# Layer 1's second mixer product as 8 × 7 Strassen products instead of 16 plain ones

## The chip, the cores and the metric

The kernel runs on one core of a Trainium2 chip. The time is the device time of one execution in microseconds (us); the time before is the median of three runs. A profiled execution has a span (first to last instruction), a little shorter than its own time.

Five engines work side by side, each on its own queue in order: PE (TensorE) multiplies, with its weight loads listed as PEld; DVE (VectorE), ACT (ScalarE) and POOL (GpSimd) work element by element; SP issues DMA transfers. SBUF is the memory on the chip and PSUM the one that PE writes its sums to.

## The reference

x has 2048 tokens × 512 channels. Twice over, attention is added to x and then a token mixer, both on a layer norm of x:

```python
x = x + _A_ref(_layernorm(x), wq, wk, wv, wo)
x = x + _B_ref(_layernorm(x), w1, b1, w2, b2)

def _B_ref(x, w1, b1, w2, b2):
    h = _layernorm(x)                                # (B, S, D)
    u = jnp.einsum("bsd,sf->bdf", h, w1) + b1        # (B, D, F)
    u = _gelu(u)
    y = jnp.einsum("bdf,fs->bds", u, w2) + b2        # (B, D, S)
    return y.transpose(0, 2, 1)
```

S is 2048, D 512, F 1792. The second mixer product is out[s,d] = sum over f of w2[f,s]·u[f,d]: 16 token tiles of 128 and 14 inner tiles of 128.

## The kernel before

All is float32. A matmul operand is split into a high part (rounded to PE's fast format, fp32r) and a low part (the rest); of each product three terms are kept: high·high, high·low and low·high. So every split is a cast (high, mostly ACT) and a subtraction (low, DVE or POOL), and every tile pair costs three matmuls.

**First mixer product** (u before the gelu). Its w1 tiles come in 128 KB loads (`load1`, SP, L1160), are cast on ACT (L1168) and get their low part on POOL (L1170). The sums go from PSUM into the tiles `ua0` to `ua13` by DVE adds (L1191). `rest` does what is left of it after the attention: behind each product `following` splits the w1 tile three ahead and loads the one seven ahead. Once an `ua` tile is complete, its gelu follows on ACT (L1389), the cast of the result on ACT (L1390), and the low part on DVE (L1394). These pieces stand between the products, by a count of turns. At its opening `rest` also issues the first two loads of w2 on SP.

**Second mixer product.** For each of the 16 token tiles, `second` does 14 × 3 = 42 matmuls of 128×128 weights against 512 columns (L1423) into one PSUM bank. w2 comes in halves of a token tile, 128×896, 448 KB each (`load2`, L1403), two buffers; `split2` casts (ACT, L1411) and subtracts (DVE, L1412) one half at a time, three buffers. One DVE instruction adds the bank and b2 to x (L1429), and SP writes the tile out.

The order of instructions on each engine is the order in which this code calls them; nothing reorders it later.

Of the kernel before, what the change touches and what calls it, by code (L numbers as in the profile page):

```python
# [8 lines left out]
F32 = mybir.dt.float32  # L9
# [9 lines left out]
P = 128  # L19
# [28 lines left out]
NP = 8  # L48
NMORE = 4
NQ = 2  # L50

VROWS = ((KR, 0, HALF - KR), (HALF + KR, HALF - KR, DH - HALF + KR))
SHIFT = 0.515625
# [13 lines left out]
def kernel(  # L67
# [993 lines left out]
    class Mixer:  # L1061
# [21 lines left out]
        def open(self):  # L1083
            n = self.l
            self.opened = True
            self.ap = pool(f"uacc{n}")
            self.wp = pool(f"w1p{n}")
            self.hp = pool(f"hp{n}")
            self.uacc = [self.ap.tile([P, D], F32, tag=f"ua{f}", name=f"ua{n}_{f}") for f in range(NF)]

        def norm(self, ts_):

# [152 lines left out]
        def rest(self, att):  # L1245
# [83 lines left out]
            att.pp.release()  # L1329
            self.open_u()  # L1330
            warm(AF.Gelu_apprx_tanh)
            self.load2(0)
            self.load2(1)
            for k, pu in enumerate(going):
                self.product(pu, start=False, stop=False)
                self.following()
                if k in (5, 7):
                    self.split2((k - 5) // 2)
            late, begun, turns = [], [], iter(range(2 * NF))

# [32 lines left out]
            for g in late:  # L1373
                self.gelu(g)
                self.gelu_rest(g)
            self.split2(2)
            self.hp.release()
            self.wp.release()
            self.ap.release()

        def open_u(self):
            n = self.l
            self.up = pool(f"up{n}", side="right")
            self.w2p = pool(f"w2p{n}", side="right")
            self.u = [self.up.tile([P, 2, D], F32R, tag=f"u{f}", name=f"u{n}_{f}") for f in range(NF)]

        def gelu(self, f):
            tmp = self.uacc[f]
            nc.scalar.activation(tmp, tmp, AF.Gelu_apprx_tanh, bias=b1c[:, f : f + 1])  # L1389
            nc.scalar.copy(self.u[f][:, 0, :], tmp)  # L1390

        def gelu_rest(self, f):
            tmp = self.uacc[f]
            nc.vector.tensor_tensor(self.u[f][:, 1, :], tmp, f32(self.u[f][:, 0, :]), op=ALU.subtract)  # L1394


# [37 lines left out]
            self.split2(2 * s + 4)  # L1434

        def close(self):
            self.w2p.release()
            self.up.release()

# [110 lines left out]
    for layer in range(2):  # L1550
# [4 lines left out]
        if more:  # L1555
            warm(AF.Exp)
            proj = Proj(layer + 1)
        for s in range(NKT):
            b = s // 4 - 1
            if more and s >= 1:  # L1560
                proj.stat(s - 1)
            if more and s >= 4 and s % 4 == 0:
                proj.spreads(tiles(b))
                proj.scales(tiles(b))
                proj.norm(tiles(b))
            if more and s == NKT - 1:
# [5 lines left out]
            if not more:  # L1572
                nc.sync.dma_start(xout[:, s, :], x[s])
                continue
# [121 lines left out]
```

## Time and profile before

| | |
|---|---|
| Median of 3 runs | 2527.39 us (2527.11 to 2529.62) |
| The profiled execution, its own time | 2527.02 us |
| Its span; outside the span | 2525.3 us; 1.7 us |
| Mean granted TensorE clock | 0.999 |
| Busy: PE / ACT / DVE / POOL | 2503.4 / 2106.1 / 1507.8 / 151.6 us |
| Layer 1's second product: first matmul to the end of the last | 2369.13 to 2521.51 us |

All times below are of this profiled execution, from the start of its span. The shares over the whole span say little here: the attention fills most of it, and the change is in the last 6%. That stretch is to be read by itself: its chain of waits, its groups of instructions, and the busy time of each engine in each part of it.

### The profile page before, as it was taken

What the parts mean: (1) busy time and instruction counts of PE and PEld (TensorE: products, weight loads), DVE (VectorE), ACT (ScalarE), POOL (GpSimd) and SP (SyncE); (2) the same over time, 40 slices, a digit from 0 to 9 for tenths busy, and PEclk for the clock granted to TensorE, in tenths of its full rate; (3) what the DMA queues carried; (4) which work ended last, traced back from release to release, by engine and by line L of the source; (5) the groups of instructions that cost most, each with busy time, mean ns of one, the idle gap of its engine ahead of it and who ended that gap; (6) DMA issues with size and microseconds to landing.
All of it is one profiled execution on the core that took longest, in us unless ns stands there. A gap on an engine that the chain in (4) does not pass through costs nothing. (4 is left out here: it accounts for less than half of the span.)

```text
span 2525.3 us, 41882 instructions
## 1 busy us (share of the span) xinstructions
PE 2503.4 (99%) x16158; PEld 1238.5 (49%) x16158; DVE 1507.8 (60%) x2406; ACT 2106.1 (83%) x2350; POOL 151.6 (6%) x239
## 2 busy tenths in 40 slices
PE   9999999999999999999999999999999999999999
PEld 6444334444444444588864433344444444436887
DVE  6565566667666776464445662666676566755532
ACT  6999999999999999653349999999999999995511
POOL 5000000000000000241000000000000000002300
PEclk9999999999999999999999999999999999999999
DMA  3221201111111110134422210111111111102343
GB/s 116 74 66 41 65 27 41 31 41 31 39 31 39 31 41 28 43 111 115 125 77 83 58 49 29 31 39 30 41 31 39 31 43 33 39 22 66 110 124 95
DMA packets 168275, 139.33 MB, mean 55 GB/s; under 512 B 17506, under 2 KB 132224, under 8 KB 167808
## 3 DMA queue, kind: packets, MB, share of 16 engines
q1 hardware_dynamic: 168064, 136.52, 18.5%
q8 instruction: 131, 2.15, 0.4%
q14 instruction: 80, 0.66, 0.1%
HBM read 95.57 MB, written 24.12 MB: 47 GB/s over the span
## 5 line engine op out<-in xcount | busy, mean ns | idle before, releaser
L906 ACT ACTIVATE p<-sc 128x1024 f32<-128x1024 f32 x1479 | 1434.4, 1048 | 68.1 <-PE sc L896 67.4
L912 PE MATMUL acc<-p,vaug 128*32 128x512 f32 x8192 | 1005.4, 599 | 0.4 <-DVE q L519 0.4
L904 DVE COPY p<-sc 128x1024 f32<-128x1024 f32 x569 | 696.7, 1224 | 475.1 <-PE sc L896 422.7
L896 PE MATMUL sc<-qs,kst 51*128 51x512 f32 x4096 | 690.2, 433 | 10.8 <-SPq L618 5.0
L906 ACT ACTIVATE p<-p 128x1024 f32<-128x1024 f32 x569 | 615.2, 1081 | 12.3 <-DVE p L904 7.3
L896 PEld LDWEIGHTS sc<-qs,kst 51*128 51x128 f32 x4096 | 335.8, 184 | 580.4 <-ACT p L906 395.4
L912 PEld LDWEIGHTS acc<-p,vaug 128*32 128x32 f32 x8192 | 218.6, 109 | 485.5 <-issue 470.0
L1423 PE MATMUL py<-u,w 128*128 128x512 f32 x1344 | 307.6, 390 | 0.0
L1423 PEld LDWEIGHTS py<-u,w 128*128 128x128 f32 x1344 | 251.8, 188 | 52.4
L1411 ACT CAST w<-w2r 128x896 fp32r<-128x896 f32 x64 | 60.3, 945 | 186.3 <-PE py L1423 178.1
L1183 PE MATMUL pu<-hb,w 128*128 128x512 f32 x768 | 204.5, 407 | 0.0
L1170 POOL TENSOR_TENSOR w<-w1r,w 128x256 fp32r<-128x256 f32 x90 | 73.5, 825 | 1648.6 <-ACT w L1168 1648.2
L1183 PEld LDWEIGHTS pu<-hb,w 128*128 128x128 f32 x768 | 136.2, 188 | 58.4 <-issue 31.7
L814 DVE COPY ev<-acc 128x512 f32<-128x512 f32 x64 | 43.9, 686 | 166.5 <-PE acc L912 166.5
L1412 DVE TENSOR_TENSOR w<-w2r,w 128x896 fp32r<-128x896 f32 x64 | 72.3, 1130 | 112.3 <-ACT w L1411 112.1
L832 DVE RECIPROCAL o<-o 128x128 f32<-128x128 f32 x120 | 113.4, 945 | 9.6 <-DMA o<-ev 9.6
L873 PE MATMUL po<-wo,hl 128*128 128x512 f32 x360 | 100.5, 412 | 2.3 <-DVE x L881 0.6
L406 PE MATMUL pq<-hT,wq 128*128 128x512 f32 x336 | 87.6, 404 | 0.0
L1168 ACT CAST w<-w1r 128x256 fp32r<-128x256 f32 x90 | 35.7, 406 | 52.8 <-PE pu_l L1183 14.2
L873 PEld LDWEIGHTS po<-wo,hl 128*128 128x128 f32 x360 | 62.6, 188 | 35.0 <-DVE x L881 12.2
L1183 PE MATMUL pu_l<-hb,w 128*128 128x512 f32 x336 | 77.5, 390 | 0.1
L1429 DVE SCALAR_TENSOR_TENSOR x<-py,b2c,x 128x512 f32<-128x512 f32 x32 | 24.0, 750 | 81.5 <-PE py L1423 81.5
(189 smaller groups left out, 1178.2 us busy)
## 6 DMA issues: line engine op xcount, KB each, us to landing
w1r<-in_B_w_dram SPq DMA_DIRECT2D x224, 128.0 KB
w2r<-in_B_w_dram SPq DMA_DIRECT2D x64, 448.0 KB
qs<-qd SPq DMA_DIRECT2D x384, 64.0 KB
qd<-q SPq DMA_DIRECT2D x64, 256.0 KB
o<-ev SPq DMA_DIRECT2D x128, 128.0 KB
x<-in_A_x_dram SPq DMA_DIRECT2D x16, 256.0 KB
out_dram<-x SPq DMA_DIRECT2D x16, 256.0 KB
wqr<-in_A_wq_dram SPq DMA_DIRECT2D x4, 512.0 KB
```

The costliest lines, as they stand in the source:

```text
L406: yield nc.tensor.matmul(out, a, c, start=(k == 0), stop=(k == len(terms) - 1))
L832: nc.vector.reciprocal(o[:, 1, c], o[:, 1, c])
L873: nc.tensor.matmul(po, a, c, start=(k == 0), stop=(k == 3 * len(parts) - 1))
L896: nc.tensor.matmul(sc[:, j, :], kst[kt // 4][rows, kt % 4 * P : (kt % 4 + 1) * P], qs[i % NQ][rows, j0 // 2, :], start=True, stop=True,)
L904: nc.vector.tensor_copy(pt, sc)
L906: nc.scalar.activation(pt, sc, AF.Exp, scale=0.25)
L912: nc.tensor.matmul(self.acc[i][c : c + 32, :], vaug[:, kt].rearrange("p d k -> p (d k)"), pt[:, j, :], start=(kt == 0), stop=(kt == NKT - ...
L1170: eng.tensor_tensor(w[:, 1], raw, f32(w[:, 0]), op=ALU.subtract)
L1183: nc.tensor.matmul(pu, a, c, start=(start and k == 0), stop=(stop and k == 5))
L1411: nc.scalar.copy(w[:, 0], raw)
L1412: nc.vector.tensor_tensor(w[:, 1], raw, f32(w[:, 0]), op=ALU.subtract)
L1423: nc.tensor.matmul(py, a, d, start=(c == 0 and f == 0 and k == 0), stop=(c == 1 and f == NFH - 1 and k == 2),)
```

## The change

It is in layer 1 only; layer 0 keeps the code above. Two token tiles (rows), the even and odd inner tiles, and the two halves of the 512 columns make a 2 × 2 × 2 block product, which is done by seven block products in place of eight (the variant with few additions).

- **Operands.** The 14 `ua` tiles become slices of two tiles, `both[0]` for even and `both[1]` for odd inner tiles. The column halves of these are the quarters b11, b12 (even) and b21, b22 (odd).
- **u's side, once.** After each gelu one half is cast and split (L1431, L1606). Behind each odd tile, `quarters` does four DVE subtractions of 128×256 (L1446 to L1449), in place and into a spare tile, and `end_second` splits one result (ACT L1437, DVE L1438) into freed attention tiles. The other four operands, t1, t3, b22 and t4, are split wide, 7 × 256 columns at a time (ACT L1455; L1456 on DVE, for b22 on POOL), when the seven products have begun.
- **w2's side, per pair of token tiles.** Four quarter loads a11, a12, a21, a22 of 448 KB (SP, L1471); four sums of them, s1 to s4, on POOL (L1475, 128×896); seven splits (ACT L1502, DVE L1503). Of the first pair, the four loads, three splits and the four sums are done within `rest`, at the turns in `EARLY`.
- **Products.** `seventh` does 7 inner pairs × 3 terms = 21 matmuls of 128×128 weights against 256 columns (L1517); 8 pairs × 7 products make 1176. `gain` adds the seven results into x: 11 DVE instructions and one ACT copy of 128×256 per pair.
- Of the gelus in `rest`, three in five turns now take one; before it was two in three.

```diff
+EARLY = (1, 3, 6, 9, 12, 15, 17)
...
-            self.load2(0)
-            self.load2(1)
+            if n == 0:
+                self.load2(0)
+                self.load2(1)
+            else:
+                for which in ("a22", "a21", "a11", "a12"):
+                    self.quarter(0, which)
...
-                ahead = late.pop(0) if next(turns) % 3 and late else None
+                turn = next(turns)
+                ahead = late.pop(0) if (turn % 3 if n == 0 else turn % 5 not in (0, 3)) and late else None
+                if n == 1 and turn in EARLY:
+                    (self.s1, self.first_split, self.s3, self.s2, self.first_split, self.first_split, self.s4)[
+                        EARLY.index(turn)
+                    ]()
...
+        def quarters(self, i):
...
+            nc.vector.tensor_tensor(b11, b12, b11, op=sub)
+            nc.vector.tensor_tensor(t2, b22, b11, op=sub)
+            nc.vector.tensor_tensor(b12, b22, b12, op=sub)
+            nc.vector.tensor_tensor(b21, b21, t2, op=sub)
+            self.split_second = i
+
+        def wide(self, e, k, out, eng=nc.vector):
+
+            raw = self.both[e][:, :, k * HD : (k + 1) * HD]
+            nc.scalar.copy(out[:, :, 1, :], raw)
+            eng.tensor_tensor(out[:, :, 0, :], raw, f32(out[:, :, 1, :]), op=ALU.subtract)
...
+        def combine(self, out, a, b, op):
+            nc.gpsimd.tensor_tensor(out, a, b, op=op)
...
+        def first_split(self):
...
+            which = ("a11", "a12", "a11", "s1", "a21", "a12", "a22")[k % 7]
+            raw = self.raws[which][-1 if which != "a22" else 0]
+            w = self.w2p.tile([P, 2, NPAIR, P], F32R, tag="w2", bufs=3, name=f"w2_{self.l}_{k}")
+            nc.scalar.copy(w[:, 0], raw)
+            nc.vector.tensor_tensor(w[:, 1], raw, f32(w[:, 0]), op=ALU.subtract)
...
+            for i in steps:
+                if p < 2:
+                    b = self.b1[:, i, p]
+                else:
+                    b = self.t2[i] if p == 2 else (self.t1, self.t3, self.b22, self.t4)[p - 3][:, i]
+                for t, (a, c) in enumerate(((0, 1), (0, 0), (1, 1))):
+                    nc.tensor.matmul(
+                        out, w[:, a, i], b[:, c, :], start=(i == 0 and t == 0),
+                        stop=(i == NPAIR - 1 and t == 2),
+                    )
...
+                    if ends:
+                        self.gain(*ends)
+                    if j == 0 and p in (0, 1):
+                        self.wide(0, p, (self.t1, self.t3)[p])
+                    if j == 0 and p == 1:
+                        self.wide(1, 1, self.b22, nc.gpsimd)
+                    if j == 0 and p == 3:
+                        self.last_quarter()
+                    if j or p:
+                        self.first_split()
...
+                    elif p == 4:
+                        self.quarter(j + 1, "a12")
+                        if j + 1 < NKT // 2:
+                            self.s1()
+                    elif p == 5 and j + 1 < NKT // 2:
+                        self.s3()
+                    elif p == 6 and j + 1 < NKT // 2:
+                        self.s2()
+                    if j == 0 and p < 2:
+                        self.seventh(k, outs[p], steps[:-1] if p == 0 else steps[:-1])
+                        if p == 1:
+                            self.seventh(0, outs[0], steps[-1:])
+                            self.gain(0, 0, outs)
+                            self.seventh(1, outs[1], steps[-1:])
```

**Three places in the order.** The first is SP's queue where `rest` opens the second product (w1r are loads of w1, w2r of w2 halves, a22 to a12 the quarters). Before:

```order
L1160 DMA w1r1_90_23502<-in_B_w1_dram 128x2x128
L1403 DMA w2r1_0_23580<-in_B_w2_dram 128x7x128
L1403 DMA w2r1_1_23582<-in_B_w2_dram 128x7x128
L1160 DMA w1r1_91_23593<-in_B_w1_dram 128x2x128
L1160 DMA w1r1_92_23604<-in_B_w1_dram 128x2x128
```

and with the change:

```order
L1171 DMA w1r1_90_23490<-in_B_w1_dram 128x2x128
L1471 DMA a22_1_0_23556<-in_B_w2_dram 128x7x128
L1471 DMA a21_1_0_23558<-in_B_w2_dram 128x7x128
L1471 DMA a11_1_0_23560<-in_B_w2_dram 128x7x128
L1471 DMA a12_1_0_23562<-in_B_w2_dram 128x7x128
L1171 DMA w1r1_91_23573<-in_B_w1_dram 128x2x128
```

Four loads of 448 KB stand ahead of the rest of w1's loads where two stood.

The second is ACT's queue from the last gelu on. Before:

```order
L1389 ACTIVATE ua1_13_14957<-ua1_13_14957,b1c_94 128x512
L1390 CAST u1_13_23577<-ua1_13_14957 128x512
L1411 CAST w2_1_2_23941<-w2r1_2_23653 128x896
L1411 CAST w2_1_3_23971<-w2r1_3_23680 128x896
L1411 CAST w2_1_4_23998<-w2r1_4_23944 128x896
```

and with the change:

```order
L1426 ACTIVATE ua1_1_14945<-ua1_1_14945,b1c_94 128x512
L1431 CAST b1_1_23552<-ua1_1_14945 128x256
L1437 CAST qs1_90<-vaug_88 128x256
L1455 CAST t1_1_23972<-ua1_0_14944 128x7x256
L1455 CAST t3_1_23973<-ua1_0_14944 128x7x256
L1455 CAST b22_1_23553<-ua1_1_14945 128x7x256
L1502 CAST w2_1_3_24005<-s1_1_0_23675 128x896
L1502 CAST w2_1_4_24034<-a21_1_0_23558 128x896
```

Between the last gelu and the next cast of w2 there are now a small cast and three wide ones.

The third is the end of POOL's queue, which before has this as its last instruction:

```order
L1170 TENSOR_TENSOR w1_1_111_23903<-w1r1_111_23857,w1_1_111_23903 128x256
```

and with the change goes on:

```order
L1181 TENSOR_TENSOR w1_1_111_23905<-w1r1_111_23843,w1_1_111_23905 128x256
L1475 TENSOR_TENSOR a12_1_0_23562<-a12_1_0_23562,a11_1_0_23560 128x896
L1456 TENSOR_TENSOR b22_1_23553<-ua1_1_14945,b22_1_23553 128x7x256
L1475 TENSOR_TENSOR s1_1_7_24099<-a21_1_1_24069,a22_1_1_23981 128x896
L1475 TENSOR_TENSOR a21_1_1_24069<-a11_1_1_24037,a21_1_1_24069 128x896
L1475 TENSOR_TENSOR a11_1_1_24037<-s1_1_7_24099,a11_1_1_24037 128x896
L1475 TENSOR_TENSOR a12_1_1_24097<-a12_1_1_24097,a11_1_1_24037 128x896
```

POOL, idle from there on before, has the last sum of the first pair, b22's low part, and then four sums for each pair that follows.

More of the change, by code (lines that the diff above doesn't have):

```diff
@@ new lines, in quarters @@
+        def quarters(self, i):
+            b11, b12, b21, b22 = (self.both[e][:, i, k * HD : (k + 1) * HD] for e in range(2) for k in range(2))
+            t2 = self.t2raw[:, i % 2, :]
+            sub = ALU.subtract
+            nc.vector.tensor_tensor(b11, b12, b11, op=sub)
[7 more added lines that the diff above has]
+            eng.tensor_tensor(out[:, :, 0, :], raw, f32(out[:, :, 1, :]), op=ALU.subtract)
@@ new lines, in gain, with add @@
+        def gain(self, j, p, outs):
+            def add(r, c, what, bias=False):
+                s = 2 * j + r
+                part = x[s][:, c * HD : (c + 1) * HD]
+                if bias:
+                    nc.vector.scalar_tensor_tensor(
+                        part, what, b2c[:, s : s + 1], part, op0=ALU.add, op1=ALU.add
+                    )
+                else:
+                    nc.vector.tensor_tensor(part, part, what, op=ALU.add)
+            mid = self.t2raw[:, j % 2, :]
+            out = outs[p]
+            if p < 2:
+                add(0, 0, out, p == 0)
+            elif p == 2:
+                nc.scalar.copy(mid, outs[0])
+                nc.vector.tensor_tensor(mid, mid, out, op=ALU.add)
+                add(0, 1, mid, True)
+            elif p == 3:
+                add(0, 1, out)
+                add(1, 1, out, True)
+            elif p == 4:
+                nc.vector.tensor_tensor(mid, mid, out, op=ALU.add)
+                add(1, 1, mid)
+                add(1, 0, mid, True)
+            else:
+                add(p - 5, 6 - p, out)
+                nc.sync.dma_start(xout[:, 2 * j + p - 5, :], x[2 * j + p - 5])
@@ new lines, in sevenths @@
+        def sevenths(self):
+            ends, steps = None, list(range(NPAIR))
+            for j in range(NKT // 2):
+                one, two_ = (bank2(f"p{k}{self.l}_{j}")[:, :, :HD] for k in "yz")
+                single = [bank(3 * j + k, f"pq{self.l}_{j}_{k}")[:, :HD] for k in range(3)]
+                outs = [
+                    one[:, 0, :], single[0], one[:, 1, :], two_[:, 0, :], two_[:, 1, :], single[1], single[2],
+                ]
+                for p in range(7):
+                    k = 7 * j + p
+                    if ends:
[8 more added lines that the diff above has]
+                        self.first_split()
+                    if p == 0:
+                        self.quarter(j + 1, "a22")
+                    elif p == 1 and j:
+                        self.s4()
+                    elif p == 2:
+                        self.quarter(j + 1, "a11")
+                    elif p == 3:
+                        self.quarter(j + 1, "a21")
+                    elif p == 4:
+                        self.quarter(j + 1, "a12")
[11 more added lines that the diff above has]
+                            self.seventh(1, outs[1], steps[-1:])
+                        ends = (0, 1, outs) if p else None
+                    else:
+                        self.seventh(k, outs[p], steps)
+                        ends = j, p, outs
+            self.gain(*ends)
@@ L1557 @@
             proj = Proj(layer + 1)
-        for s in range(NKT):
+        if not more:
+            mix.sevenths()
+        for s in range(NKT if more else 0):
             b = s // 4 - 1
-            if more and s >= 1:
+            if s >= 1:
                 proj.stat(s - 1)
-            if more and s >= 4 and s % 4 == 0:
+            if s >= 4 and s % 4 == 0:
                 proj.spreads(tiles(b))
@@ L1565 @@
                 proj.norm(tiles(b))
-            if more and s == NKT - 1:
+            if s == NKT - 1:
                 proj.spreads(tiles(NB - 1)[:3])
```

95 lines of the change are left out of this document (87 added, 8 removed).

## The prediction

> **What bounds the kernel now.** I read the chain of waits first, over the stretch from 2360 us to the end.
>
> ```profile
> 2359.84 9.29 PE pu_l L1183 x41
> 2369.13 152.38 PE py L1423 x672
> 2521.51 0.02 issue
> 2521.54 0.75 DVE x L1429
> ```
>
> PE bounds it alone: 672 matmuls in 152.38 us without a wait, 226.8 ns each. Then the groups of instructions of the same stretch (count, busy us and mean ns, idle before and its releaser).
>
> ```profile
> L1423 PE MATMUL py<-u,w 128*128 128x512 f32 x672 | 152.5, 389 | 0.0
> L1423 PEld LDWEIGHTS py<-u,w 128*128 128x128 f32 x672 | 126.1, 188 | 26.2
> L1412 DVE TENSOR_TENSOR w<-w2r,w 128x896 fp32r<-128x896 f32 x30 | 32.8, 1092 | 56.4 <-ACT w L1411 56.3
> L1411 ACT CAST w<-w2r 128x896 fp32r<-128x896 f32 x30 | 28.4, 948 | 108.6 <-PE py L1423 108.6
> L1429 DVE SCALAR_TENSOR_TENSOR x<-py,b2c,x 128x512 f32<-128x512 f32 x16 | 12.0, 751 | 49.1 <-PE py L1423 49.1
> L1394 DVE TENSOR_TENSOR u<-ua,u 128x512 fp32r<-128x512 f32 x8 | 5.4, 691 | 3.5 <-ACT u L1390 3.5
> L1389 ACT ACTIVATE ua<-ua,b1c 128x512 f32<-128x512 f32 x7 | 5.1, 722 | 0.5 <-DVE ua L1191 0.5
> L1191 DVE TENSOR_TENSOR ua<-ua,pu_l 128x512 f32<-128x512 f32 x4 | 2.7, 685 | 1.0 <-PE pu_l L1183 1.0
> L1168 ACT CAST w<-w1r 128x256 fp32r<-128x256 f32 x5 | 1.9, 403 | 0.1
> ```
>
> DVE and ACT work far below PE there; their idle time ends with PE. The busy times by stretch (PE, PEld, DVE, ACT, POOL, then clock, DMA share and GB/s) show where the slack is.
>
> ```profile
> 2330.20:2341.10 10.90, 10.90 (x49) 9.01 (x48) 8.11 (x20) 5.10 (x12) 5.58 (x8) 1.00 0.60 162
> 2341.10:2369.00 27.90, 27.80 (x123) 22.61 (x122) 17.17 (x26) 21.95 (x43) 16.78 (x19) 1.00 0.40 113
> 2388.00:2502.50 114.50, 114.50 (x506) 94.81 (x506) 35.22 (x36) 22.75 (x25) 0.00 (x0) 1.00 0.42 125
> ```
>
> In the steady part DVE is busy 31% and POOL does nothing. In the 28 us ahead of it, where the gelus run, ACT is at 79%, DVE at 62%, POOL at 60%: this stretch is already full, and the change puts most of its new preparation there.
>
> **PE's own gain.** 1176 matmuls of 256 columns replace 672 of 512. At half of 226.8 ns, 113.4 ns each, that is 133.4 us in place of 152.4: 19.0 us less, 16.7 us per pair of token tiles in place of 19.05. This holds if a weight load still hides behind a matmul of half the length. The recorded loads take 188 ns, but they wait in there. The nearest row with short matmuls, each with its own load of 128 columns, is at the start (PE's timeline).
>
> ```profile
> 5.03 6.00 PE L131 MATMUL pw<-ident 128*128 128x128 f32 x32
> 10.86 2.84 PE L131 MATMUL pt<-ident 128*128 128x128 f32 x24
> 13.54 1.91 PE L377 MATMUL pt<-ident,h 128*128 128x128 f32 x16
> ```
>
> From 10.86 to 13.54 there are 24 in 2.68 us, 111.7 ns each, so loads can go at least that fast. Bounds: 111.7 ns (131.4 us) and 188 ns (221 us); I take 113.4.
>
> **Prices of the new operations.** DVE with two operands in SBUF costs 691 ns for 512 and 1092 for 896 columns: 1.044 ns per column, so 0.42 us for 256 and 2.03 for 1792. With one operand in PSUM, 685 and 751 ns less 267 make 0.42 and 0.48 for 256. ACT's casts (403 ns at 256, 948 at 896) give 1.71 us for 1792. For POOL I read its groups over the whole span.
>
> ```profile
> L1170 POOL TENSOR_TENSOR w<-w1r,w 128x256 fp32r<-128x256 f32 x90 | 73.5, 825 | 1648.6 <-ACT w L1168 1648.2
> L315 POOL TENSOR_TENSOR wq<-wqr,wq 128x256 fp32r<-128x256 f32 x4 | 2.9, 739 | 0.0
> L315 POOL TENSOR_TENSOR wq<-wqr,wq 128x512 fp32r<-128x512 f32 x2 | 2.5, 1284 | 0.0
> ```
>
> 545 ns more for 256 more columns, 2.13 ns per column: 2.10 us for 896, 4.01 for 1792.
>
> **POOL and DVE exclude one another.** The timeline shows it, first while POOL is in an operation and then while DVE is.
>
> ```profile
> 2321.10 0.16 DVE L223 TENSOR_TENSOR rw_b_l<-rw_b_l 128x2 f32<-128x2 f32 x1
> 2321.66 0.74 POOL L1170 TENSOR_TENSOR w<-w1r,w 128x256 fp32r<-128x256 f32 x1 [0.62 <-ACT w L1168]
> 2321.68 0.72 DVE L223 TENSOR_TENSOR rw_b_l<-rw_b_l 128x2 f32<-128x2 f32 x1
> 2358.28 0.69 DVE L1394 TENSOR_TENSOR u<-ua,u 128x512 fp32r<-128x512 f32 x1 [0.66 <-ACT u L1390]
> 2358.63 0.94 POOL L1170 TENSOR_TENSOR w<-w1r,w 128x256 fp32r<-128x256 f32 x1 [0.40 <-ACT w L1168]
> 2358.89 0.68 DVE L1191 TENSOR_TENSOR ua<-ua,pu_l 128x512 f32<-128x512 f32 x1
> ```
>
> A DVE operation on two columns takes 0.16 us alone and 0.72 beside POOL's: it waits for POOL's end. POOL's takes 0.94 instead of 0.74 when DVE is in one with two SBUF operands. L1191, with one operand in PSUM, is not held up (0.68). The overlap that remains is small: of the 0.34 us that both are recorded, 0.20 is POOL's delay, so 0.14 is free. The Trainium skill (SBUF — State Buffer, Who interferes with whom) has this as an exclusive lock on shared ports, for DVE instructions with two SBUF inputs against POOL instructions that read SBUF, held for the whole instruction. The rows agree. Without the lock, product 3 below would start at 2380.7 and a pair take 16.7: last matmul at 2380.7 + 9.5 + 7 × 16.7 = 2507, a time of 2512.
>
> **Steady pairs.** Locked work per pair: four sums on POOL, 4 × 2.10; seven splits on DVE, 7 × 1.09; three gains with both operands in SBUF, 1.3; together 17.3 us, over PE's 16.7. The other eight gains (3.5 us, PSUM operand) pass the lock only when they happen to stand at the head of DVE's queue during a sum. So a pair takes 17.3 to 20.8 us. DVE's queue alternates splits and gains, so I take about a third of the 3.5: 18.5 us, just under 19.05. If the free overlaps of 0.14 us, twice per sum, counted in full, it would be 16.2, and PE would decide at 16.7. For the last pair, which needs only one sum, 18. Transfers cost nothing here: a pair still loads four times 448 KB, and though a quarter has one buffer, its reload is issued a product or more before a sum reads it and several before a split does; at the 162 GB/s of the first stretch above it takes 2.8 us. If it came late, POOL's first sum would wait, whose split is four products away.
>
> **The way from the last add to the fourth product.** Before, PE went on at 2369.13 because the gelus ran ahead and three w2 tiles were split.
>
> ```profile
> 2369.17 0.69 DVE L1191 TENSOR_TENSOR ua<-ua,pu_l 128x512 f32<-128x512 f32 x1 [0.68 <-PE pu_l L1183]
> 2369.89 0.72 ACT L1389 ACTIVATE ua<-ua,b1c 128x512 f32<-128x512 f32 x1
> ```
>
> Now, with three splits made ahead, PE has products 0 to 2 ready, 3 × 2.38 us: to 2376.3. Product 3 needs t1 and the fourth split, and this lies behind, from the add's end at 2369.86: gelu 0.72, cast 0.41, low part 0.42, four quarters 1.70 (2373.1); on ACT the small cast 0.40 and three wide casts of 1.71 (2378.6); then POOL takes the lock with b22 for 4.01 (2382.6), and DVE's split, whose cast came at 2379.6, follows with 1.09: 2383.7. So PE waits at least 7.4 us, even with nothing late.
>
> **What is late.** From 2341.1 on the locked work is: on DVE 14 low parts 5.9, 28 quarters 11.8, 7 small splits 2.9, three splits 3.3, together 23.9; on POOL some 20 subtractions of 0.74 and four sums of 2.10, together 23.2. That is 47.1 us, one after the other, in a stretch of 27.9; the adds beside it (14 × 0.685) are free only where they meet POOL. Strictly it ends at 2388.2; if each of POOL's 24 operations overlaps by 0.14 at both ends, 6.7 earlier, at 2381.5. I take the middle, 2384.9, for the end of the last quarters, against 2373.1 above: 11.8 late (8.4 to 15.1), product 3 at 2395.5.
>
> ACT gets seven small casts and one of w2 more in this stretch, 3.8 us into its 5.9 of slack, so it is not what is late first.
>
> SP adds a little. The four quarter loads stand ahead of w1's loads.
>
> ```profile
> 2331.00 1.07 SPq L1403 DMA_DIRECT2D w2r<-in_B_w_dram  x2
> 2338.56 0.78 ACT L1168 CAST w<-w1r 128x256 fp32r<-128x256 f32 x2 [3.38 <-DMA w1r<-in_B_w_dram]
> ```
>
> Behind two loads a w1 cast already waited 3.38 us. Two more, 896 KB, add, at 162 GB/s, 5.5 us of transfer at most, and the first product's end loses up to that. But then the locked work waits on PE less, so I count nothing here, and +5 in the range.
>
> **The sum.** Product 3 at 2395.5; the remaining four products of the first pair 9.5, and 2.5 for the last wide split (2.03, locked) ahead of product 5's; six pairs of 18.5 and one of 18, 129. That is 2536.5. PE has then stood idle for nearly 20 us, and the first rows above show the cold price: 32 matmuls in 6.00 us, 187 ns against 112, so up to 2.4 us lost; I take 1. The Trainium skill (TensorE: Matmul & The Clock Gate, What's actually happening) puts PE at half speed after an idle window of about 3.4 us until it has been busy as long; as an estimate from that page it costs 1.7 us, no run here shows it in mid-kernel. Last matmul at 2537.5 against 2521.5: +16.0; the closing add has 256 columns, 0.42 in place of 0.75: −0.3. On the profiled execution's 2527.0 this makes 2542.7, and with the median 0.4 above that execution, 2543.
>
> **Rivals.**
> *The lock bites little and PE decides.* The free overlaps count in full, DVE's waits on ACT take the sums, and the backlog fits into the 10.7 us that DVE has left in the stretch. For it: 16.2 against 16.7 above. Against it: 47 us into 28. Then product 3 at 2383.7, 9.5, and 7 × 16.7: 2510.1, or 2515.
> *Both signs cancel.* Little backlog, but pairs of 18.5: 2383.7 + 12 + 129 = 2524.7, +3, or 2530. The stretch would have to be as empty as DVE's 62% reads.
> *Weight loads decide.* At 188 ns per matmul 1176 take 221 us, 68.7 more: 2596 and up. The 111.7 ns row speaks against it.
> *PE wins nothing, in the other sense:* that there are 1176 matmuls of 256 columns is in the code, so I give this no chance.
>
> **How the numbers follow.** 0.58 for the forecast (2531 to 2560 by its bounds: backlog 8.4 to 15.1, pairs from 17.3, or upward 3 for the backlog, 5 for the loads and the rest for longer pairs), 0.22 for PE deciding, 0.12 for cancelling, 0.08 for weight loads. The range of 8 in 10 runs from 2514, in the midst of the second case, to 2558. A measurement of this kernel can tell about 0.2%, 5 us, from no change: faster 0.22, same 0.12, slower 0.66, since the forecast's bounds end above that.
>
> **What would show it.** In the profile after: the spacing of the new matmuls (113 ns within a product); PE idle by 15 to 25 us ahead of product 3, with the DVE split as its releaser; POOL's sums above 2.10 us on average and DVE's splits above 1.09, if they lock; pairs 18 to 19 us apart; product 3 near 2395. The prediction is wrong if product 3 starts before 2388, or if pairs are 16.7 us apart: then lock and backlog were overrated.

## The result, and the profile after

The kernel with the change takes 2567.64 us (median of 4 runs, 2565.66 to 2570.78), against 2527.25 for the kernel before beside it: ratio 1.0162, 95% interval 1.0144 to 1.0179. It is 40.4 us slower. The prediction said 2543, 16 us slower: the sign was right, the loss was two and a half times as large, and 2567.64 lies outside the stated range.

The profiled execution took 2570.78 us, its span 2569.0. Ahead of the first product's tail, executions differ by some us whatever the kernel (the opening, below, comes at 2316.2 to 2323.9 us in the profiles of this case), so in what follows stretches are counted from one instruction, called the opening: the first of the 48 matmuls that begin that tail. It stands at 2319.57 us before and at 2321.61 after. From there to the end of the span are 205.7 us before and 247.4 after, +41.7.

The windows view gives the engines' busy time by stretch (window, its length, then busy time and instructions of PE, PEld, DVE, ACT, POOL, granted clock, DMA share, GB/s). First the kernel before, from the opening to the second product's first matmul and from there to its last:

```profile
2319.57:2368.97 49.40, 49.30 (x217) 40.42 (x216) 35.33 (x69) 30.72 (x62) 28.14 (x34) 1.00 0.42 118
2368.97:2521.50 152.53, 152.53 (x673) 125.94 (x671) 46.62 (x49) 30.57 (x34) 0.00 (x0) 1.00 0.37 111
```

Then with the change: the tail of the first product, the first pair of token tiles, and the six pairs after it.

```profile
2321.61:2382.42 60.81, 51.91 (x217) 40.94 (x216) 47.35 (x86) 27.36 (x61) 36.46 (x38) 0.97 0.38 107
2382.42:2425.56 43.14, 23.14 (x147) 22.04 (x148) 32.68 (x43) 17.57 (x24) 10.95 (x4) 0.76 0.12 33
2425.56:2545.25 119.69, 107.86 (x885) 105.72 (x883) 101.07 (x109) 41.15 (x48) 51.38 (x24) 1.00 0.41 117
```

The tail takes 60.8 us in place of 49.4 (+11.4), the first pair 43.1 where two plain tiles take 19.05 (+24.1), the six pairs 19.95 each on average (+5.4 in all); the rest, +0.8, is the last pair. PE, which never waited before, is busy in only 23.1 of the first pair's 43.1 us, and at a granted clock of 0.76.

What PE waited for in the second product (the waits view: engine and tile, who ended the wait, us in total, times, longest):

```profile
PE py L1517 <- DVE x L1528: 18.4, 7, 11.5
PE pz L1517 <- ACT w L1502: 7.0, 7, 1.0
PE pz L1517 <- DVE x L1528: 6.6, 1, 6.6
```

L1528 is no operand's instruction, it is a `gain`: DVE adding a finished product into x. The matmuls that wait for it are those of product 2 (in `py`, the tile that product 0 has filled) and of product 4 (in `pz`, filled by product 3). The second row is product 4 again, in the seven later pairs; the gain and the cast that is named end within 0.2 us of one another there, and e1 below tells which it is. The timeline of PE shows both in the first pair (start, us, what; in brackets the idle time before and its releaser):

```profile
2402.14 2.93 PE L1517 MATMUL py<-kst,w 128*128 128x256 f32 x12 [11.48 <-DVE x L1528]
2406.79 2.67 PE L1517 MATMUL pz<-t,w 128*128 128x256 f32 x21
2416.00 4.74 PE L1517 MATMUL pz<-t,w 128*128 128x256 f32 x21 [6.55 <-DVE x L1528]
```

and the timelines of DVE and POOL show where those gains stood:

```profile
2396.18 4.57 POOL L1456 TENSOR_TENSOR b<-ua,b 128x1792 fp32r<-128x1792 f32 x1 [16.16 <-ACT b L1455]
2396.97 4.72 DVE L1503 TENSOR_TENSOR w<-s,w 128x896 fp32r<-128x896 f32 x1
2401.62 0.47 DVE L1528 SCALAR_TENSOR_TENSOR x<-py,b2c,x 128x256 f32<-128x256 f32 x1
...
2407.92 2.11 POOL L1475 TENSOR_TENSOR s<-a,a 128x896 f32<-128x896 f32 x1 [7.18 <-DVE vaug L1540]
2407.93 2.38 DVE L1528 SCALAR_TENSOR_TENSOR x<-vaug,b2c,x 128x256 f32<-128x256 f32 x1
2410.11 2.14 POOL L1475 TENSOR_TENSOR a<-a,a 128x896 f32<-128x896 f32 x1
2410.24 3.89 DVE L1456 TENSOR_TENSOR t<-ua,t 128x1792 fp32r<-128x1792 f32 x1
2415.39 0.47 DVE L1528 SCALAR_TENSOR_TENSOR x<-pz,b2c,x 128x256 f32<-128x256 f32 x1
```

The lock is there as predicted: a split of 1.09 us takes 4.72 beside b22's operation on POOL; of the next two sums on POOL, the first stretches a gain of 0.48 to 2.38 and the second a low part of 2.0 to 3.89. But PE is not waiting for these. It waits for a gain that stands behind them in DVE's queue and that frees no operand. Product 2 writes another bank than the one that this gain reads; both are halves of one tile of two banks (`bank2`). In the program, product 4's first matmul waits for DVE and ACT, while product 3's first, whose half of the tile nobody reads at that time, waits for ACT alone.

### The profile page after: what moved, and what is told of

It is laid out like the page before. It is cut to its first block, busy times and chain, and to the rows that moved or that the text cites. A ratio compares the mean times of both kernels' runs of the same rounds, so it can differ in the third digit from the quotient of the medians.

```text
span 2569.0 us, 43203 instructions
## 1 busy us (share of the span) xinstructions
PE 2504.9 (98%) x16662; PEld 1259.1 (49%) x16662; DVE 1620.7 (63%) x2540; ACT 2136.1 (83%) x2393; POOL 226.2 (9%) x272
## 3 DMA queue, kind: packets, MB, share of 16 engines
q1 hardware_dynamic: 168064, 136.52, 18.6%
q8 instruction: 135, 2.21, 0.4%
## 5 line engine op out<-in xcount | busy, mean ns | idle before, releaser
L909 ACT ACTIVATE p<-p 128x1024 f32<-128x1024 f32 x569 | 615.1, 1081 | 11.5 <-DVE p L907 6.4
L1639 PE MATMUL py<-u,w 128*128 128x512 f32 x672 | 155.1, 390 | 0.0
L1639 PEld LDWEIGHTS py<-u,w 128*128 128x128 f32 x672 | 125.7, 188 | 26.1
L835 DVE RECIPROCAL o<-o 128x128 f32<-128x128 f32 x120 | 113.4, 945 | 10.0 <-DMA o<-ev 10.0
L1502 ACT CAST w<-a 128x896 fp32r<-128x896 f32 x48 | 45.2, 943 | 78.1 <-PE pz L1517 35.7
L1627 ACT CAST w<-w2r 128x896 fp32r<-128x896 f32 x32 | 30.0, 944 | 76.4 <-PE py L1639 68.5
L876 PEld LDWEIGHTS po<-wo,hl 128*128 128x128 f32 x360 | 62.6, 188 | 34.3 <-DVE x L884 11.7
L1503 DVE TENSOR_TENSOR w<-a,w 128x896 fp32r<-128x896 f32 x48 | 77.1, 1606 | 3.4 <-ACT w L1502 3.4
```

The costliest lines, as they stand in the source:

```text
L835: nc.vector.reciprocal(o[:, 1, c], o[:, 1, c])
L876: nc.tensor.matmul(po, a, c, start=(k == 0), stop=(k == 3 * len(parts) - 1))
L909: nc.scalar.activation(pt, sc, AF.Exp, scale=0.25)
L1503: nc.vector.tensor_tensor(w[:, 1], raw, f32(w[:, 0]), op=ALU.subtract)
L1639: nc.tensor.matmul(py, a, d, start=(c == 0 and f == 0 and k == 0), stop=(c == 1 and f == NFH - 1 and k == 2),)
```

## The experiments

Twelve kernels were run. "Later pairs" is the mean distance from one pair's third product to the next one's, from the second pair on; "first product" is the time from the opening to the second product's first matmul; all from one profiled execution each. In e9, e10 and e12 the second product begins with plain tiles. The time is the median. The runs fall into four groups, each with its own runs of the kernel before beside it (medians 2526.3 to 2528.2 us), so between groups the ratios compare better than the times.

| kernel | first product, us | later pairs, us | opening to end, us | time, us | ratio to before |
|---|---|---|---|---|---|
| before | 49.4 | 19.05 | 205.7 | 2527.25 | 1 |
| the change | 60.8 | 20.17 | 247.4 | 2567.64 | 1.0162 |
| e1 tiles dealt anew | 60.5 | 19.76 | 233.6 | 2551.89 | 1.0096 |
| e2 no sums | 54.7 | 18.67 | 227.7 | 2551.39 | 1.0090 |
| e3 no quarters | 54.9 | 20.15 | 235.0 | 2557.15 | 1.0117 |
| e4 late loads | 57.3 | 20.15 | 244.2 | 2565.39 | 1.0146 |
| e5 = e1 and e2 | 55.2 | 17.41 | 211.2 | 2532.31 | 1.0023 |
| e6 = e1, b22 on DVE | 60.2 | 19.69 | 230.9 | 2553.67 | 1.0110 |
| e7 = e1, sums earlier | 60.9 | 17.83 | 221.7 | 2542.32 | 1.0061 |
| e8 = e7, e6 and e4 | 58.1 | 17.85 | 217.3 | 2538.39 | 1.0046 |
| e11 sums earlier alone | 59.2 | 23.77 | 263.4 | 2585.74 | 1.0222 |
| e9 two plain pairs | 49.0 | 17.65 | 200.7 | 2523.42 | 0.9984 |
| e10 three plain pairs | 49.1 | 17.95 | 202.8 | 2525.82 | 0.9994 |
| e12 t4 earlier | 49.0 | 17.79 | 199.6 | 2523.16 | 0.9984 |

**e1: the PSUM tiles dealt out anew.** The theory after the result: products 2 and 4 wait only because of the tile that they share. The rival: lock and splits are the chain, and the waits just show it.

```diff
-                    one[:, 0, :], single[0], one[:, 1, :], two_[:, 0, :], two_[:, 1, :], single[1], single[2],
+                    one[:, 0, :], single[0], single[1], two_[:, 0, :], single[2], one[:, 1, :], two_[:, 1, :],
```

> Only the PSUM tiles of the seven products are dealt out anew: in the change products 0 and 2 share a tile of two banks, and so do 3 and 4; here 0 and 5 share one, and 3 and 6, so that no product shares a tile with one whose gain comes just before it. Theory 'shared tile': product 2 waits for the gain of product 0, and product 4 for the gain of product 3, only because they stand in one tile. Then the 1.0 us of PE idle ahead of product 4 and the 1.15 us ahead of product 2 go, pairs come down from 20.2 to 18.0 to 18.6 us (what lock and matmuls leave), the 6.6 us ahead of product 4 in the first pair go too, and the time falls by 15 to 22 us, to about 2549. Rival 'lock alone': POOL's sums and DVE's splits are the chain, the waits only show it; pairs stay at 20 us or more and the time falls by less than 4 us.

Measured: 2551.89 us, 15.7 less, from one line that moves no arithmetic. The first pair now has its third product at 68.5 us after the opening (80.5 before the edit), its fourth at 75.0 (where it stops after two matmuls and goes on at 79.8, when its split is there), and takes 31.4 us in place of 43.1. The shared tile is thus shown as a cause. Most of what it cost lies in the first pair: 11.7 of the 13.8 us that the profile shows from the opening to the end. The later pairs, however, stay at 19.76, nearer to the rival's 20 than to the 18.0 to 18.6 expected. PE's waits in them have moved to the splits:

```profile
PE pq L1517 <- DVE w L1503: 5.1, 9, 1.6
PE py L1517 <- DVE w L1503: 0.7, 2, 0.4
PE pq L1517 <- ACT w L1502: 0.5, 1, 0.5
```

**e2: no sums.** The 32 sums s1 to s4 on POOL are left out; the products are then not those of the reference. With the sums go their lock and every wait for a sum, so this run does not tell the two apart.

```diff
         def combine(self, out, a, b, op):
-            nc.gpsimd.tensor_tensor(out, a, b, op=op)
+            pass
```

> Leaves out all of POOL's sums s1 to s4 (32 operations of 128x896); the splits read the quarters as they were loaded. So in the steady pairs POOL never takes the lock. 'Shared tile': pairs come to 18.6 to 18.9 us, since product 4 still waits 1.0 us for the gain of product 3; with some 6 us won ahead of the first pair the time falls by about 16, to 2552. 'Lock alone': pairs come to 17.5 (147 matmuls of 119 ns), PE has no wait left in them, and the time falls by 25 us or more.

Measured: 2551.39 us, pairs of 18.67, both as the shared tile has it. Without any sum in the pairs, PE still waits once in each, ahead of product 4 (PE's timeline; the gain of product 3 and the cast that is named end at nearly the same time):

```profile
2441.78 2.63 PE L1515 MATMUL pz<-t,w 128*128 128x256 f32 x21
2445.40 2.71 PE L1515 MATMUL pz<-t,w 128*128 128x256 f32 x21 [1.00 <-ACT w L1500]
```

**e3: no quarters.** The 28 subtractions behind the gelus are left out, so the operands are other ones than Strassen's.

```diff
-            nc.vector.tensor_tensor(b11, b12, b11, op=sub)
-            nc.vector.tensor_tensor(t2, b22, b11, op=sub)
-            nc.vector.tensor_tensor(b12, b22, b12, op=sub)
-            nc.vector.tensor_tensor(b21, b21, t2, op=sub)
```

> Leaves out the 28 DVE subtractions of 128x256 behind the gelus (quarters); the operands are split from the raw quarters, all else stays. Theory 'backlog': the first product ends at 2381.5 instead of 2369.1 because its adds stand in DVE's queue behind locked work; with 11.8 us less of it, the first product ends near 2372, and the time falls by 9 to 12 us. Rival: the w1 loads, which come late behind the four quarter loads, and ACT hold the first product back; then its end moves by less than 4 us.

Measured: 2557.15 us, 10.5 less, as expected of the backlog; the first product ends only 5.9 us earlier, where some 9.5 were expected. So DVE's work does hold the first product back, by way of its adds, which free the PSUM banks. In e2 four sums less on POOL give 6.1 us in the same stretch. That these act through the lock is in the change's own trace: DVE waits there for no sum, but four of its operations of 0.42 us, each beside a sum, take 1.71 to 2.35, like this one:

```profile
2358.40 2.35 DVE L1448 TENSOR_TENSOR ua<-ua,ua 128x256 f32<-128x256 f32 x1
2358.16 2.31 POOL L1475 TENSOR_TENSOR a<-a,a 128x896 f32<-128x896 f32 x1
```

With both runs the backlog is shown.

**e4: a11 and a12 loaded later.**

```diff
-                for which in ("a22", "a21", "a11", "a12"):
+                for which in ("a22", "a21"):
...
+                if n == 1 and turn in (0, 5):
+                    self.quarter(0, "a12" if turn else "a11")
```

> Only a22 and a21 are loaded at the opening of the second product; a11 follows at turn 0 and a12 at turn 5, so that w1's loads stand behind two loads of 448 KB as before. The 3.0 us of PE idle at 2342 us, which end with a w1 cast, go. Theory 'backlog': the locked work still sets the end of the first product, and the time falls by 0 to 2 us. Rival 'loads': it falls by 3 us or more.

Measured: 2565.39 us. The medians differ by 2.3 us, the first product ends 3.5 us earlier and the whole stretch is 3.2 shorter. That lies between the two, nearer to the rival: the wait behind the two additional loads is not absorbed by the backlog, it adds to it. The times alone do not show this, since the intervals of the two ratios overlap (1.0130 to 1.0163 and 1.0144 to 1.0179); but e8 beside e7, which has the same edit among others, shows the first product 2.8 us shorter too.

**e5: both the tiles and the sums.** Is there a third cause in the pairs?

> Both edits at once: the PSUM tiles dealt out anew as in the first run, and all of POOL's sums s1 to s4 left out. Theory 'shared tile and lock, nothing else': with both gone PE is the only bound in the steady pairs, 147 matmuls at the 119 ns that the profile after shows, 17.5 to 17.7 us per pair in place of 19.7 with the tiles dealt anew alone and 18.7 without sums alone; the time is about 2551.9 less 7 x 2.1 less 6 for the stretch ahead, 2531. Rival: something else keeps the pairs above 18.2 us (weight loads, DVE's splits, transfers), and the time stays above 2536.

Measured: 2532.31 us, pairs of 17.41; PE waits for nothing in them. This is also the price of the new matmul by itself, 17.41 / 147 = 118.4 ns. Products follow one another without a gap:

```profile
2440.72 2.68 PE L1515 MATMUL pq<-b,w 128*128 128x256 f32 x21
2443.24 1.57 PE L1515 MATMUL pq<-kst,w 128*128 128x256 f32 x12
...
2455.61 2.67 PE L1515 MATMUL py<-b,w 128*128 128x256 f32 x21
2458.12 2.68 PE L1515 MATMUL pq<-b,w 128*128 128x256 f32 x21
```

So 17.41 is the floor, 18.67 with the shared tile alone, 19.76 with the sums alone, called where the change calls them, and 20.17 with both: the causes overlap rather than add.

**e6: b22's low part on DVE**, on top of e1.

```diff
-                        self.wide(1, 1, self.b22, nc.gpsimd)
+                        self.wide(1, 1, self.b22)
```

> On top of the tiles dealt out anew, b22's low part of 7 x 256 columns is made on DVE instead of POOL. With the tiles dealt anew PE still waits 3.9 and 4.0 us ahead of and within product 3 of the first pair, the second time for the DVE split that b22's operation on POOL (4.6 us in the trace) holds up. Theory 'b22 holds the lock': 2.0 us on DVE in place of 4.6 on POOL, and the time falls by 2 to 3 us from 2551.9, to about 2549. Rival 'DVE's queue': the wide low parts on DVE are the chain by themselves, and it does not fall, or rises by up to 2 us.

Measured: 2553.67 us, beside 2551.89 for e1; ratios 1.0110 (1.0093 to 1.0127) and 1.0096 (1.0079 to 1.0113), no difference that can be told. In the profiles the stretch is 2.8 us shorter, as the theory has it. The times do not confirm that; it stays open.

**e7: the sums called earlier**, on top of e1: why do four sums of 2.1 us cost 2.3 us in each pair, when splits and sums together hold the lock for less than a pair? In e1's trace s1 waits for its load of a21 and then all four sums follow within 12 us. Besides the lines shown, a21 gets a second buffer.

```diff
-                        self.quarter(j + 1, "a22")
+                        self.quarter(j + 1, "a21")
+                        self.quarter(j + 1, "a22")
...
-                    elif p == 3:
-                        self.quarter(j + 1, "a21")
+                    elif p == 3 and j + 1 < NKT // 2:
+                        self.s1()
                     elif p == 4:
                         self.quarter(j + 1, "a12")
-                        if j + 1 < NKT // 2:
-                            self.s1()
```

> On top of the tiles dealt out anew, a21 gets a second buffer, its load goes out at the pair's first product instead of the fourth, and POOL's sum s1 is called one product earlier. With the tiles dealt anew s1 waits for its load, and all four sums then stand within 12 us, each in turn with a DVE split. Theory 'bunched sums': spread out, the lock fits beside the matmuls, pairs come down from 19.7 to about 18 us, and the time from 2551.9 to about 2540. Rival 'sum of holds': what the lock holds in all, 17.3 us and the gains that DVE can't do meanwhile, sets the pair wherever the sums stand; pairs stay above 19.2 us and the time above 2548.

Measured: 2542.32 us and pairs of 17.83, the numbers expected of bunched sums; the rival is excluded. But the mechanism is another than the expectation says, because the sums are hardly spread. Here are the first and the last sum of one pair, and the third product of that pair and of the next, in e1:

```profile
2455.00 0.40 PE L1517 MATMUL pq<-kst,w 128*128 128x256 f32 x2
2463.15 2.13 POOL L1475 TENSOR_TENSOR s<-a,a 128x896 f32<-128x896 f32 x1 [8.31 <-DVE w L1503]
2472.18 2.12 POOL L1475 TENSOR_TENSOR a<-a,a 128x896 f32<-128x896 f32 x1 [1.08 <-issue]
2474.48 0.40 PE L1517 MATMUL pq<-kst,w 128*128 128x256 f32 x2
```

and in e7:

```profile
2453.44 1.92 PE L1517 MATMUL pq<-kst,w 128*128 128x256 f32 x12
2458.03 2.55 POOL L1475 TENSOR_TENSOR s<-a,a 128x896 f32<-128x896 f32 x1 [5.15 <-DMA a<-in_B_w_dram]
2468.55 2.13 POOL L1475 TENSOR_TENSOR a<-a,a 128x896 f32<-128x896 f32 x1 [1.08 <-issue]
2471.26 1.87 PE L1517 MATMUL pq<-kst,w 128*128 128x256 f32 x12
```

The four sums stand within 9.8 to 12.2 us in e1 and within 12.2 to 13.1 in e7. What has changed more is where they begin: s1 starts 4.2 to 5.1 us after the third product in place of 7.5 to 10.2. POOL works no less: s1 takes 2.63 us on average (2.24 in e1), and in both kernels the splits that meet a sum take 2.96 us. But they now end before PE needs them: PE's waits of 6.3 us in the 100 us from 2425 on (e1's rows above) have shrunk to one of 0.2. Begun early, all four sums and their collisions cost 17.83 − 17.41 = 0.4 us per pair. That the early begin does it, and not the little spreading, is read from these traces; no run separates the two.

**e8: four edits together** (e7, e6, e4).

> Four edits together: tiles dealt anew, a21's second buffer, b22 on DVE, and a11 and a12 loaded later in the first product. If they act on different stretches they add up: about 3 us for the loads (seen alone), 2.5 for b22 and 12 for the sums, from 2551.9 to about 2534. If the backlog of locked work in the first product takes the place of what is removed, it stays above 2542.

Measured: 2538.39 us, between the two outcomes, 4 us above the sum; from the opening 217.3, 4.4 less than e7 (about 3 of it the loads'). In all 11.6 us are still lost: 8.7 in the first product and 11.6 in the first pair (30.7 us in place of 19.05), of which the seven later pairs win back 1.2 us each.

**e11: the earlier sums alone**, with the PSUM tiles as in the change, to complete the square of the two causes.

> a21's second buffer and the earlier s1 alone, with the PSUM tiles as in the change. Theory 'two causes side by side': the shared tile keeps its 1.0 us ahead of product 4 in each pair, as it did without sums (18.7 us), so pairs come to about 18.7 to 19 from 20.2; the first pair stays at 43 us; the time falls by 8 to 10 us, to about 2558. Rival: bunched sums alone set the pairs, and they come to 17.8; then it falls by 16 us or more.

Measured: 2585.74 us, 18 us slower than the change itself, pairs of 23.77. Both expectations were wrong, and the timelines say why (PE, DVE and POOL around one product 4):

```profile
2453.00 2.63 PE L1517 MATMUL pz<-t,w 128*128 128x256 f32 x21
2459.44 4.82 PE L1517 MATMUL pz<-t,w 128*128 128x256 f32 x21 [3.82 <-DVE x L1528]
```

```profile
2454.06 1.63 DVE L1528 SCALAR_TENSOR_TENSOR x<-vaug,b2c,x 128x256 f32<-128x256 f32 x1
2455.61 2.96 DVE L1503 TENSOR_TENSOR w<-a,w 128x896 fp32r<-128x896 f32 x1
2458.49 0.41 DVE L1532 TENSOR_TENSOR x<-x,pz 128x256 f32<-128x256 f32 x1
2458.82 0.47 DVE L1528 SCALAR_TENSOR_TENSOR x<-pz,b2c,x 128x256 f32<-128x256 f32 x1
```

```profile
2453.27 2.14 POOL L1475 TENSOR_TENSOR s<-a,a 128x896 f32<-128x896 f32 x1 [5.16 <-DMA a<-in_B_w_dram]
2455.48 2.14 POOL L1475 TENSOR_TENSOR a<-a,a 128x896 f32<-128x896 f32 x1
```

The earlier sums meet exactly the DVE operations that stand ahead of product 3's gain, and since product 4 waits for that gain, their lock lands on PE: 3.82 us idle. After such an idle time the 21 matmuls take 4.82 us instead of 2.63. The last pair, beside which no sums are made, waits 1.00 us at this place, as in e2. The same edit wins 9.6 us with the tiles dealt anew (e7 beside e1) and loses 18 without.

**e9, e10, e12: the first pairs plain.** If tail and first pair lose 35 us and a later pair wins 1.2, the preparation belongs beside plain matmuls. Here the first two pairs (e9) or three (e10) are done as before the change; quarters, t1 and the first sums are made beside their matmuls, the quarters are then loaded only where they are needed, and the later pairs are e7's. J0 is the number of plain pairs.

```diff
+            for s in range(2 * J0):
+                mix.plain(s)
             mix.sevenths()
...
-            for j in range(NKT // 2):
+            for j in range(J0, NKT // 2):
```

> The first two pairs of token tiles (four tiles) are done as before the change, and only the six pairs after them by seven products, with the tiles dealt anew and a21's second buffer. The first product's tail is then as before the change: two w2 loads, gelus on 512 columns, no quarters and no sums in it. The quarters, t1 and the first sums (some 25 us on DVE) are made beside the plain tiles' 38 us of matmuls, t3 in the place of u's freed halves. If the loss of the change lies in the first product's tail and the first pair (11 and 24 us) as the traces show, and the late pairs take 17.8 us in place of 19.05, this wins 6 x 1.25 = 7.5 us less a us or two where the two kinds meet: 2520 beside 2526.5 before, ratio 0.9975. Rival: the work moved beside the plain tiles holds their splits back, PE waits there, and the time comes out at 2528 or more.

> As the run above with three plain pairs and five pairs by seven products, the preparation still beside the last two plain ones. It wins 1.25 us less, 2521, if every late pair is worth 1.25 us; if the place where the two kinds meet costs most, both come out alike.

Measured: e9 2523.42 us, ratio 0.9984 (0.9975 to 0.9993), faster than the kernel before by a little more than the interval; e10 2525.82, ratio 0.9994 (0.9985 to 1.0003), not to be told from it. From the opening they are 5.0 and 2.9 us shorter than before. e9 won less than the 6.5 us expected (2520 beside 2526.5), and e10 missed its 2521. Four plain tiles run without a wait, and then one wait is left, in the first pair by seven products:

```profile
2367.70 38.29 PE L1644 MATMUL py<-u,w 128*128 128x512 f32 x168
2421.00 3.60 PE L1506 MATMUL py<-u,w 128*128 128x256 f32 x19 [2.30 <-DVE w L1489]
```

t4's low part stood ahead of the split that this product needs. e12 moves it to a place behind an earlier split.

```diff
-                    if j == J0 and p == 3:
-                        self.last_quarter()
                     if j > J0 or p:
                         self.first_split()
+                    if j == J0 and p == 2:
+                        self.last_quarter()
```

> As the run with two plain pairs, only that t4 (a wide cast and a low part of 7 x 256 columns) is made behind the split at the third product of the first pair by seven products, not ahead of the split at the fourth. There its low part (2.0 us, 3.95 with the lock) stood ahead of the split that product 5 needs, and PE waited 2.3 us and ran cold for a moment after. If that is right, this wait goes and the time falls by 2 to 3.5 us, ratio to before 0.997. If the lock with the sums only moves the wait to another product, it stays at 0.9984.

Measured: 2523.16 us, ratio 0.9984 (0.9975 to 0.9993): no gain that can be told, as the other outcome has it. The wait is still there, and t4's low part still takes twice its 2.0 us beside POOL's sums:

```profile
2417.33 3.94 DVE L1435 TENSOR_TENSOR t<-ua,t 128x1792 fp32r<-128x1792 f32 x1
```

## Why the prediction was right or wrong, point by point

**PE's own gain** was put at 113.4 ns per matmul; e5 shows 118.4. Half the columns are a little more than half the time. Over 1176 matmuls that is 5.9 us less to win. The weight loads do not set this price at their recorded length: their records still read 188 ns or more at a spacing of 118. Whether they have a part in the 5 ns above half, no run shows; the row of 111.7 ns, taken for a lower bound, is of 128 columns in plain float32 (`ident`) and says little of a matmul of 256 columns in fp32r.

**The lock** was read rightly, and its prices hold in the change's groups (line, engine, operation, shapes and count; busy us and mean ns; idle before):

```profile
L1503 DVE TENSOR_TENSOR w<-a,w 128x896 fp32r<-128x896 f32 x48 | 77.1, 1606 | 3.4 <-ACT w L1502 3.4
L1503 DVE TENSOR_TENSOR w<-s,w 128x896 fp32r<-128x896 f32 x8 | 12.2, 1531 | 0.1
L1475 POOL TENSOR_TENSOR a<-s,a 128x896 f32<-128x896 f32 x8 | 17.2, 2145 | 21.1 <-DVE w L1503 21.1
L1475 POOL TENSOR_TENSOR s<-a,a 128x896 f32<-128x896 f32 x8 | 18.9, 2362 | 58.6 <-DMA a<-in_B_w_dram 43.7 <-DVE x L1528 7.7 <-DVE vaug L1540 7.2
L1456 DVE TENSOR_TENSOR t<-ua,t 128x1792 fp32r<-128x1792 f32 x3 | 7.9, 2645 | 1.1 <-ACT t L1455 1.1
```

2.1 to 2.4 us for a sum, where 2.10 was estimated, and splits that go from 1.09 to 1.6 on average, as announced among the signs. The rule of the Trainium skill that was weighed there (SBUF — State Buffer, Who interferes with whom) agrees with the rows shown: in e11's trace a split of 1.08 us that meets a whole sum takes 2.96.

**The first product's tail** was expected late by its backlog, with the last quarters 65.3 us after the opening (2384.9); they ended at 70.0, a little past the upper bound. In this the step on SP failed in part: "I count nothing here" for the loads, but they cost 3.5 us of their own (e4), on top of the backlog and not inside it.

**The way to the fourth product** was computed to 75.9 us after the opening (2395.5). In e1, where no tile interferes, the split that decides it is there at 79.8, late by about as much as the quarters; in the change the product starts at 85.2. **The step that failed** is the next term of the sum: "the remaining four products of the first pair 9.5, and 2.5 for the last wide split". It took products to wait for operands only. So did, ahead of it, "PE has products 0 to 2 ready": product 2 had its operands (in e1 it runs right behind product 1), and PE stood idle 11.5 us before it. The waits that a PSUM tile brings with it were nowhere in the list, though the diff shows `one[:, 0, :]` and `one[:, 1, :]` given to products two apart. The pair ended 104.0 us after the opening instead of the predicted 87.9. These 16 us, of the 26 by which the forecast was short (41.7 against 15.7), are the shared tile's 11.7 (43.1 less e1's 31.4) and some 4 by which the first pair ends late in e1 too, as the quarters do.

**The pairs** were put at 18.5 us within bounds of 17.3 and 20.8, and measured 20.17. The bounds held, the choice between them did not, and with the last pair this is the other 11 us (140 us from the first pair's end to the last matmul, against 129); the 1 us put in for the clock stands against it. Two sentences were wrong there. "Transfers cost nothing here": the s1 of five of the seven later pairs waits for its load (the 43.7 us of the row above). The prediction had weighed a late load only by s1's own split, "four products away"; but the other sums follow s1, and the split for the next pair's third product reads one of them. Called earlier, with a second buffer for a21, the sums are worth 1.9 us a pair less once the tiles are dealt anew (e7). And the lock was summed as if whatever it holds up were late; begun early, the same sums cost 0.4 us.

**The rivals.** That PE decides (pairs of 16.7) would have needed both e1's and e7's edits, and comes to 17.8 then. That both signs cancel fails in the first product alone, which lost 11.4 us. That weight loads decide, at 188 ns per matmul, is excluded by e5's 118.4.

**The signs** given in advance: PE idle ahead of product 3 "with the DVE split as its releaser" was wrong in a telling way: the releaser was a gain, and ahead of product 2. **The clock** was put at 1 us; the change's first pair has two cold stretches, product 2 in 4.65 us and product 4 in 4.58, from each start to the next product's, in place of 2.5; so some 4.2 us.

## What to carry to other kernels

Before costing a change that has more products in flight, list for each of them not only the operands but also what its output tile shares, and where the reader of its neighbour stands in the queue of its engine; a wait of this kind turns every hold-up on that engine into idle time of PE. A count of locked time does not say what the lock costs: the same four sums, called at the same place in the program, cost 0.4 us per pair (e7 beside e5) or 5.1 (e11 beside e2), depending on whether PE waited for what they held up. And an algorithm that saves a steady 1.2 us per step has to have its preparation hidden beside work of the old kind: the two versions with two plain pairs ahead (e9 and e12) were the only ones tried that won, by 0.16% each.

## What the runs showed of the hardware beyond that

PE's granted clock falls after short idle times in mid-kernel. In e11 each idle time of 3.3 to 4.4 us is followed by 21 matmuls in 3.9 to 4.8 us instead of 2.6 (granted clock 0.50 in the 4.6 us from 2459.44 on); after 1.0 us (e2) they take their usual time, and after 2.2 to 2.3 us it went both ways: 3.60 us for 19 matmuls in e9, and in e10 and then e12, after idle times that differ by 0.02 us:

```profile
2444.20 3.98 PE L1506 MATMUL py<-u,w 128*128 128x256 f32 x19 [2.21 <-DVE w L1489]
2424.57 2.53 PE L1506 MATMUL py<-u,w 128*128 128x256 f32 x19 [2.19 <-DVE w L1489]
```

So a wait of 4 us costs PE about 6. The Trainium skill (TensorE: Matmul & The Clock Gate, What's actually happening) states half speed after an idle window of about 3.4 us. The longer of these waits agree with it; those of 2.21 and 2.30 us that ran cold are shorter than that window, so the length of the wait alone does not decide here.

A matmul of 128x128 weights takes 226.8 ns for 512 columns and 118.4 for 256 when PE never waits: drawn through these two points, 0.42 ns per column and 10 ns that do not depend on them. No run has a third width to test that line.
